# Expert stage as one row of 256-token blocks: nine fixed, the rest read from a table made on the chip

## The chip, the cores and the metric

The kernel runs on one core of one Trainium2 chip. The metric is the device time of one execution in microseconds (us). Three executions of the kernel before took 937.12, 929.86 and 933.24 us, median 933.24 us. Engine names are those of the profile: PE (matrix products; PEld is its weight load), DVE (vector), ACT (scalar), POOL (the engine that also issues gathers and scatters), SP (the queue that issues plain transfers).

## What is computed

```python
# 1: a recurrent layer over 768 steps (4 x 8 heads of 48), output x of 3072 tokens x 384
# 2: x = relu(x @ w_in) ** 2 @ w_out                       (384 -> 2048 -> 384)
# 3: the expert layer
skip_score = x @ w_skip
do_compute = skip_score > 0
out = x.copy()
xc = x[do_compute]
logits = xc @ w_gate                                       # 8 experts
e_idx = np.argmax(logits, axis=1)
gate_w = softmax(logits)[arange, e_idx]
for e in range(8):
    mask = e_idx == e
    h = np.maximum(xc[mask] @ w1[e], 0.0)                  # 384 -> 1024
    y[mask] = gate_w[mask, None] * (h @ w2[e])             # 1024 -> 384
out[do_compute] = xc + y
```

How many tokens an expert gets is known only on the chip. With the inputs of this case the eight experts get 1155, 132, 435, 318, 112, 43, 143 and 59 tokens, worked out from the reference; the other 675 of 3072 are passed through.

## The kernel before, in words

The first 651 us are the recurrent layer and the dense layer, laid over each other; the change leaves their code alone. While the dense layer runs, each token is routed: its number and its gate are scattered to a list per expert in memory (`lst`, two halves, merged by `merge` into `lsb` on the chip). The first entries of expert 0's list are read early (`lsp`), so that its first block can start before the lists are whole.

The expert stage works on **blocks**. A block is one expert's weights times up to 256 (`body256`) or 128 (`body128`) tokens of its list. Its parts:

- `gather`: POOL fetches the tokens' rows of x by index, 128 at a time, into `xg`. `xprep` turns them round on PE and splits them into a high and a low part (ACT the high, DVE the low).
- `l1(f)`, f = 0 to 7: nine products of 256 columns (three passes over high and low parts) into one of four PSUM banks; ACT makes the relu, DVE the low part of the hidden values (`gl`). `l2(f)`: for each half of the tokens three products of 384 columns into `acc[t]`. `l2(f)` stands four steps behind `l1`.
- `finish`: DVE multiplies by the gate and adds x (`yo`), POOL scatters the rows to `out`.
- The weights: SP loads an expert's weights as eight pieces of 384 KB into `raw` (`ew_load`), and ACT or DVE with DVE or POOL split each piece into high and low (`ew_split`). There are two sets of split weights and two `raw` buffers. While a block of expert e runs, the weights of e + 1 are split and those of e + 2 loaded, piece by piece at places that the table `CTP` sets.

Which blocks run is decided at run time: after each block every engine tests the expert's count (`large`, line 949: is there another 256; `level`, line 956: more than 128 left or not). The first block of expert 0 is outside these tests. With the counts above the order is: expert 0 five blocks of 256; expert 1 one; expert 2 two; expert 3 one of 256 and one of 128; experts 4 and 5 one of 128 each; expert 6 one of 256; expert 7 one of 128. So ten blocks of 256 and four of 128. At the very end a flag is tested (line 991) that redoes two blocks of expert 0 if the early list was not whole; with these inputs it is not set.

Of the kernel before, what the change touches and what calls it, by code (L numbers as in the profile page):

```python
# [83 lines left out]
def rwkv_moe_kernel(ctx: ExitStack, tc: tile.TileContext, a_in, v_in, ud, wio,  # L84
# [7 lines left out]
    xtd = dram.tile([NB * 4, 96, S], F32, name="xtd")  # L92

# [31 lines left out]
    flg = per.tile([1, 2], I32, name="flg")  # L125
# [496 lines left out]
    def ew_piece(e, k):  # L622

        r = raws[e > 0 and e % 2 == 0][:, k]
        w1h, w1l, w2h, w2l = ew[e % 2]
        if k < 4:
            s = slice(256 * k, 256 * k + 256)
            return r, r.rearrange("p (k f) -> p k f", k=KC), w1h[:, :, s], w1l[:, :, s]
        s = slice(2 * (k - 4), 2 * (k - 4) + 2)
        return r, r.rearrange("p (j d) -> p j d", j=2), w2h[:, s], w2l[:, s]  # L630

    def ew_load(e, k):
        nc.sync.dma_start(raws[e > 0 and e % 2 == 0][:, k], we[e, k])

    def ew_split(e, k, eng, dv=0):
        _, r, h, l = ew_piece(e, k)
        (nc.vector.tensor_copy if dv else nc.scalar.copy)(h, r)  # L637
        eng.tensor_tensor(l, r, h.bitcast(F32), ALU.subtract)
# [93 lines left out]
    NLV = NTOK // UT  # L732
    xgs = [[cp.tile([128, DM], F32, name=f"xg0_{t}") for t in range(2)]]
    yos = [cp.tile([128, DM], F32, name=f"yo{i}") for i in range(2)]
    ptx = [ptk, pu]
    nyo = [0]
    xhs, xls = list(xth), list(xtl)

    def xbuf(e, k):
        return 2 if k % 2 else e % 2  # L740

    def gbuf(e, k):
        return 3 if k % 2 else e % 3

    def ids(e, k, t):
        c = e * LB + 2 * k + t
        return lsb[:, c, 0:1], lsb[:, c, 1:2].bitcast(F32)

    def ids0(e, k, t):
        return lsp[0][:, 2 * k + t, 0:1], lsp[0][:, 2 * k + t, 1:2].bitcast(F32)  # L750
# [9 lines left out]
    def gather(e, k, idf=ids):  # L760
        for t in range(2):
            nc.gpsimd.indirect_dma_start(
                xgs[gbuf(e, k)][t], None, x2d[:, :],
                bass.IndirectOffsetOnAxis(ap=idf(e, k, t)[0], axis=0),
                bounds_check=NTOK + PADR - 1, oob_is_err=False)

    def xprep(e, k, t):
        i = xbuf(e, k)
        bank = ptx[t]
        for kc in range(KC):  # L770
            nc.tensor.transpose(bank[:, kc * 128:(kc + 1) * 128], xgs[gbuf(e, k)][t][:, kc * 128:(kc + 1) * 128], ident)
        s = slice(t * 128, t * 128 + 128)
        src = bank[:, 0:DM].rearrange("p (k t) -> p k t", k=KC)
        nc.scalar.copy(xhs[i][:, :, s], src)
        nc.vector.tensor_tensor(xls[i][:, :, s], src, xhs[i][:, :, s].bitcast(F32), ALU.subtract)

    def finish(e, k, t, idf=ids):
        ix, gt = idf(e, k, t)
        y = yos[nyo[0] % len(yos)]
        nyo[0] += 1  # L780
        nc.vector.scalar_tensor_tensor(y, acc[t][:, 0:DM], gt, xgs[gbuf(e, k)][t], ALU.mult, ALU.add)  # L781
        nc.gpsimd.indirect_dma_start(  # L782
            out[:, :], bass.IndirectOffsetOnAxis(ap=ix, axis=0), y, None,
            bounds_check=NTOK - 1, oob_is_err=False)
# [6 lines left out]
    at(TB + 10, 3, lambda: gather(0, 0, ids0))  # L791
    for t in range(2):
        at(TB + 13 + t, 1, lambda t=t: xprep(0, 0, t))
# [7 lines left out]
    xls.append(cq.tile([128, KC, UT], F32R, name="cxl2"))  # L801
    hps = pgs + [[cq.tile([128, UT], F32R, name=f"{n}{i}") for n in ("gh", "gl")] for i in range(NPB, LAG + 1)]
    ls2 = cq.tile([128, NE * LB, 2], I32, name="ls2")
    hrs = cq.tile([128, FE], F32, name="hr")
    hth, htl = ([hps[d][z].rearrange("p (j t) -> p j t", j=2) for d in range(4)] for z in range(2))
    pb = [t.rearrange("p (j t) -> p j t", j=4)
          for t in (pat.rearrange("p a b c -> p (a b c)"), py.rearrange("p a b -> p (a b)"))]
    l1b = [ph[0], ph[1], pat.rearrange("p a b c -> p (a b c)"), py.rearrange("p a b -> p (a b)")]

    def hook(side, n):  # L810
        for v, m in sorted((v, m) for m, (v, _) in enumerate(side) if n <= v < n + 1):
            side[m][1]()

    def body256(e, k, side, idf=ids):

        w1h, w1l, w2h, w2l = ew[e % 2]
        xh, xl = xhs[xbuf(e, k)], xls[xbuf(e, k)]
# [13 lines left out]
        def l2(f):  # L831
            hh, hl = hps[f % (LAG + 1)]
            for t in range(2):
# [16 lines left out]
        for t in range(2):  # L850
            finish(e, k, t, idf)

    def body128(e, k, side):
        w1h, w1l, w2h, w2l = ew[e % 2]
        xh, xl = xhs[xbuf(e, k)], xls[xbuf(e, k)]

        def l1(z, ns):
            s = slice(512 * z, 512 * z + 512)
            for n in ns:
                kc, (a, w) = n % 3, ((xh, w1h), (xh, w1l), (xl, w1h))[n // 3]  # L860
                nc.tensor.matmul(ph[z], a[:, kc, 0:128], w[:, kc, s], start=(n == 0), stop=(n == 3 * KC - 1))
            if ns[-1] == 3 * KC - 1:
                nc.scalar.activation(hrs[:, s], ph[z], AF.Relu)

        def turn(z):
            for j in range(4):
                f = 4 * z + j
                nc.tensor.transpose(pb[j // 2][:, j % 2], hrs[:, f * 128:(f + 1) * 128], ident)
            for m in range(2):
                d = 2 * z + m  # L870
                src = pb[m][:, 0:2]
                (nc.vector.tensor_copy if d == 1 else nc.scalar.copy)(hth[d], src)
                nc.vector.tensor_tensor(htl[d], src, hth[d].bitcast(F32), ALU.subtract)

        def l2(f):
            for n, (a, w) in enumerate(((hth, w2h), (hth, w2l), (htl, w2h))):
                nc.tensor.matmul(acc[0][:, 0:DM], a[f // 2][:, f % 2], w[:, f, :],
                                 start=(f == 0 and n == 0), stop=(f == NJE - 1 and n == 2))

        hook(side, 0)  # L880
        l1(0, range(0, 9))
        hook(side, 1)
        l1(1, range(0, 5))
        turn(0)
        hook(side, 2)
        l1(1, range(5, 9))
        hook(side, 3)
        l2(0)
        l2(1)
        turn(1)  # L890
        hook(side, 4)
        l2(2)
        hook(side, 5)
        l2(3)
        l2(4)
        hook(side, 6)
        for f in range(5, 8):
            l2(f)
        hook(side, 7)
        finish(e, k, 0)  # L900

    def sides(e, k, full):
        side = []

        def add(v, f):
            side.append((v, f))

        if full and k + 1 < NLV:
            add(CTP["g"][2], lambda: gather(e, k + 1))
            add(4, lambda: hint(f"n{e}_{k}", counts[e] > UT * (k + 1)))  # L910
        if k == 0 and e + 2 < NE:
            add(CTP["g"][full], lambda: gather(e + 2, 0))
        if k == 0 and e + 1 < NE:
            splits(side, e + 1, int(full))
        if e + 1 < NE:
            add(3.5, lambda: hint(f"s{e + 1}_0", counts[e + 1] > 128))
        for t in range(2):
            if k == 0 and e + 1 < NE:
                add(CTP["x"][full][t], lambda t=t: xprep(e + 1, 0, t))
            if (e, k) == (0, 1):  # L920
                add(CTP["x"][1][t], lambda t=t: xprep(1, 0, t))
            if full and k + 1 < NLV:
                add(CTP["x"][2][t], lambda t=t: xprep(e, k + 1, t))
        return side

    def splits(side, e, m):
        for p in range(8):
            def f(p=p):
                ew_split(e, p, nc.gpsimd if CTP["e"][m][p] else nc.vector, CTP["h"][m][p])
                if e + 2 < NE and m < 2:  # L930
                    ew_load(e + 2, p)
            side.append((CTP["l"][m][p], f))
            if m == 2:
                side.append((0.01, lambda p=p: ew_load(2, p)))
                side.append((max(4, CTP["l"][m][p] + 0.001), lambda p=p: ew_load(3, p)))
# [145 lines left out]
```

## Time and profile before

| | |
|---|---|
| median of three runs | 933.24 us (929.86 to 937.12) |
| the profiled execution | 937.27 us, its span 935.4 us, so 1.9 us lie outside the span |
| PE busy | 825.9 us, 88% of the span |
| DVE, ACT, POOL busy | 562.7, 450.6, 558.3 us |
| mean granted PE clock | 0.968 of full |
| expert stage on PE | 651.0 to 920.5 us |

The span runs from the first to the last instruction. A busy PE is not PE at its peak, so a block is best measured from the start of its first product to the start of the next block's. "PEclk" in a window is the clock granted to PE as a share of full: it has two levels, 1.2 and 2.4 GHz, and a value between is a mix over the window.

### The profile page before, as it was taken

Reading aid. Unit: us, or ns where it says so; the run is one execution under the profiler, and the core shown is the slowest. Engines: PE = TensorE matmul, PEld = TensorE weight load, DVE = VectorE, ACT = ScalarE, POOL = GpSimd, SP = SyncE. Lnnn points to the kernel's source line nnn. Section 1 sums busy time; section 2 is a strip of 40 time slices with the busy share of each in tenths; the row PEclk is TensorE's granted clock in tenths of the full one; section 3 lists DMA queues with packets and bytes.
Section 4 is the critical chain, followed back from the end, with each engine's and each line's share of the span. In section 5 each row is a group of like instructions: output and inputs, shape, how many; then the busy total and the mean of one; then the engine's idle time right before and its main releaser. Section 6 shows DMA issues by size and latency. Waiting matters only on the chain. (4 is left out here: it accounts for less than half of the span.)

```text
span 935.4 us, 17875 instructions
## 1 busy us (share of the span) xinstructions
PE 825.9 (88%) x6528; PEld 774.8 (83%) x6528; DVE 562.7 (60%) x1222; ACT 450.6 (48%) x1160; POOL 558.3 (60%) x603
## 2 busy tenths in 40 slices
PE   2574899999999999999999999989989989897873
PEld 2454788999999999999999999988979978886773
DVE  6986962658576767666667676325622357265651
ACT  1342565665656656666566556556312233144330
POOL 7765876767676767667676767335741254254440
PEclk9999999999999999999999999989999998999787
DMA  7454322232223131313232311055921145253310
GB/s 191 144 171 117 131 59 51 77 76 76 68 59 84 43 84 43 85 42 85 43 84 47 94 36 48 11 189 167 308 88 49 35 153 185 69 185 102 99 32 6
DMA packets 56639, 86.84 MB, mean 93 GB/s; under 512 B 31476, under 2 KB 40840, under 8 KB 56480
## 3 DMA queue, kind: packets, MB, share of 16 engines
q1 hardware_dynamic: 49104, 72.53, 27.2%
q0 software_dynamic: 4736, 11.18, 3.8%
q10 hardware_dynamic: 2640, 1.23, 0.6%
q8 instruction: 72, 1.18, 0.5%
q14 instruction: 87, 0.71, 0.3%
HBM read 68.44 MB, written 15.16 MB: 89 GB/s over the span
## 5 line engine op out<-in xcount | busy, mean ns | idle before, releaser
L364 POOL TENSOR_TENSOR gl<-g,gh 128x256 fp32r<-128x256 f32 x192 | 149.3, 779 | 144.4 <-ACT gh L363 99.7
L356 PE MATMUL ph<-xt,wih 128*128 128x256 f32 x1152 | 228.6, 294 | 4.2 <-PEq L719 3.8
L356 PEld LDWEIGHTS ph<-xt,wih 128*128 128x128 f32 x1152 | 184.6, 193 | 8.6 <-issue 4.3
L356 PE MATMUL ph<-xt,wil 128*128 128x256 f32 x576 | 164.2, 285 | 0.0
L372 PE MATMUL acc<-woh,gl 128*128 128x394 f32 x384 | 132.7, 346 | 0.7 <-POOL gl L364 0.7
L372 PE MATMUL acc<-woh,gh 128*128 128x394 f32 x384 | 133.0, 346 | 0.0
L361 ACT ACTIVATE g<-ph 128x256 f32<-128x256 f32 x192 | 72.8, 379 | 124.7 <-PE ph L356 97.3
L372 PE MATMUL acc<-wol,gh 128*128 128x394 f32 x384 | 131.0, 341 | 0.0
L356 PEld LDWEIGHTS ph<-xt,wil 128*128 128x128 f32 x576 | 111.0, 193 | 0.0
L287 DVE COPY_PREDICATED gr<-cis,pat 64x256 f32<-64x256 int32 x192 | 85.5, 445 | 32.9 <-PE pat L277 28.7
L782 POOL DMA_INDIRECT out<-yo,lsb x22 | 22.7, 1033 | 111.5 <-DVE yo L781 71.6
L362 ACT ACTIVATE g<-g 128x256 f32<-128x256 f32 x192 | 80.2, 418 | 6.1
L363 ACT CAST gh<-g 128x256 fp32r<-128x256 f32 x192 | 77.9, 406 | 6.1
L372 PEld LDWEIGHTS acc<-woh,gl 128*128 128x128 f32 x384 | 72.3, 188 | 4.2 <-POOL gl L364 3.9
L372 PEld LDWEIGHTS acc<-woh,gh 128*128 128x128 f32 x384 | 72.7, 189 | 0.7
L372 PEld LDWEIGHTS acc<-wol,gh 128*128 128x128 f32 x384 | 72.9, 190 | 0.0
L277 PE MATMUL pat<-ru,kbd 112*128 112x128 f32 x384 | 56.6, 295 | 14.7 <-POOL kbd L250 14.5
L277 PEld LDWEIGHTS pat<-ru,kbd 112*128 112x128 f32 x384 | 53.9, 209 | 15.2 <-POOL kbd L250 14.5
L221 DVE STREAM_TRANSPOSE knd<-kbd 32x256 f32<-32x256 f32 x144 | 62.4, 434 | 3.5 <-POOL kbd L250 1.1
L250 POOL TENSOR_TENSOR kbd<-ain,bsc 48x512 f32<-48x512 f32 x48 | 59.2, 1233 | 3.2 <-DVE bsc L215 0.7
L836 PE MATMUL acc<-w2h,gh 128*128 128x384 f32 x160 | 57.5, 359 | 0.0
L329 PEld LDWEIGHTS py<-gr,vz 128*64 128x64 f32 (+2 forms) x768 | 33.5, 144 | 28.0 <-ACT vz L320 12.8
(214 smaller groups left out, 1781.0 us busy)
## 6 DMA issues: line engine op xcount, KB each, us to landing
raw<-in_we SPq DMA_DIRECT2D x64, 384.0 KB
ain<-in_a_in SPq DMA_DIRECT2D x23, 675.9 KB
raw<-in_wio SPq DMA_DIRECT2D x16, 768.0 KB
vz<-in_v_in SPq DMA_DIRECT2D x44, 128.0 KB
x2d<-x SPq DMA_DIRECT2D x12, 384.0 KB
out<-x SPq DMA_DIRECT2D x12, 384.0 KB
xt<-yt SPq DMA_DIRECT2D x72, 32.0 KB
ain<-in_a_in ACTq DMA_DIRECT2D x1, 675.9 KB
```

What stands on the lines that cost most here:

```text
L221: nc.vector.transpose(kn[64 * h + 32 * b2:64 * h + 32 * b2 + 32, :, :, 64 * h + 32 * a:64 * h + 32 * a + 32], kb[64 * h + 32 * a:64 * h + ...
L250: eng("lk", H).tensor_tensor(st["kb"][sl, :, :, 64 * h:64 * h + 64], k[sl], st["rc"][sl], ALU.mult)
L277: nc.tensor.matmul(pat[:, c], kb[0:112, qq, c, :], ru[:, qq, c], start=True, stop=True)
L287: nc.vector.copy_predicated(gr[sl, qq, :, h, :], msk[sl].unsqueeze(1).to_broadcast([64, 4, CH]), pat[sl, :, m, :])
L329: nc.tensor.matmul(py[64 * h:64 * h + 64, P % 2, c * CH:(c + 1) * CH], hv[H][ks, qq, c, h, :], gr[ks, qq, c, h, :], start=True, stop=True)
L356: nc.tensor.matmul(h[:, 0:UT], w[:, kc, j * 128:(j + 1) * 128], x[:, kc, :], start=(n == 0), stop=(n == 3 * KC - 1))
L361: nc.scalar.activation(g, h[:, 0:UT], AF.Relu)
L362: nc.scalar.activation(g, g, AF.Square)
L363: nc.scalar.copy(gh, g)
L364: nc.gpsimd.tensor_tensor(gl, g, gh.bitcast(F32), ALU.subtract)
L372: nc.tensor.matmul(acc[t][:, 0:OW], a[:, s], w[:, j, :], start=(j == 0 and n == 0), stop=(j == NJ - 1 and n == 2))
L836: nc.tensor.matmul(acc[t][:, 0:DM], a[:, s], w[:, f, :], start=(f == 0 and m == 0), stop=(f == NJE - 1 and m == 2))
```

## The change

The branches on every expert's count go. The expert stage becomes one row of blocks, all of 256 tokens. Nine are fixed: two of expert 0 (from the early list) and one of each other expert. All that is left over (`rest`) is up to twelve further blocks; a table of their expert and list place is computed by 25 small DVE operations in block 1 (`table`), and block n of the rest runs if the table has more than n entries. The test stands nested, one level deeper for each block, and is true for five blocks with these counts: experts 0, 0, 0, 2, 3.

The weights of block n + 1 are always split during block n and those of block n + 2 always loaded, for the rest with the expert's number read from the table into a register of SP, so expert 0's weights are loaded and split three times more. The last four `l2` steps of a block are now done for the first 128 tokens, then for the second, so that the first half can be finished earlier; the second half's scatter waits until the next block in the fixed row. `xg`, x and `yo` take turns by block number. The order of loads in block 0 changes: the lists first, then the eight pieces of the second weight set.

```diff
 CTP = {
-    "l": [[0, 0.1, 0.2, 1.7, 2.2, 3.2, 4.5, 5.5], [0.4, 1.2, 2.0, 2.8, 3.6, 4.4, 5.2, 6.0],
...
+    "l": [0.3, 1.2, 2.1, 3.0, 3.9, 4.4, 5.9, 6.7],
+    "e": [0, 1, 0, 0, 1, 0, 1, 0],
+    "x": [5.1, 5.6],
+    "s": 1.6,
+    "g": 2.6}
+NX = NTOK // UT
+NST = NE + 1
...
+    def ew_load(n, k, ex=None):
+
+        src = we[n, k] if ex is None else we[bass.ds(ex, 1), k].rearrange("o p f -> (o p) f")
+        nc.sync.dma_start(raw(n)[:, k], src)
...
-        (nc.vector.tensor_copy if dv else nc.scalar.copy)(h, r)
+        nc.scalar.copy(h, r)
         eng.tensor_tensor(l, r, h.bitcast(F32), ALU.subtract)
...
+    def wset(n):
+
+        return max(n - 1, 0)
+
+    def ids(n, t):
+        if n < 2:
+            l = lsp[0][:, 2 * n + t]
+        elif n < NST:
+            l = lsb[:, (n - 1) * LB + t]
+        else:
+            l = idt[:, n - NST, t]
+        return l[:, 0:1], l[:, 1:2].bitcast(F32)
...
+    def table():
+
+        V = nc.vector
...
+        V.tensor_scalar(ti[:, 0], cnt[0:1], 1, None, ALU.subtract)
+        V.tensor_scalar(ti[:, 1], ti[:, 0], 8, None, ALU.arith_shift_right)
...
+        V.tensor_tensor_scan(cx, cfs[0:1, 256:256 + NE], ex, 0.0, ALU.mult, ALU.add)
+        V.tensor_copy(nbk, cx[:, NE - 1:NE])
...
+        V.tensor_copy(tbl[:, 0], eb)
+        V.tensor_copy(tbl[:, 1], kb)
+
+    def ex_load(b):
+        exr[b] = nc.values_load(tbl[0:1, 0, b:b + 1], engines=[mybir.EngineType.SP], min_val=0, max_val=NE - 1)
+
+    def id_load(b):
+        c = nc.values_load(tbl[0:1, 1, b:b + 1], engines=[mybir.EngineType.SP], min_val=0, max_val=NE * LB - 2)
+        nc.sync.dma_start(idt[:, b], lm[:, bass.ds(c, 2), :])
...
-        for f in range(NJE + LAG):
-            if f < NJE:
-                steps.append(lambda f=f: l1(f))
+        for f in range(NJE):
+            steps.append(lambda f=f: l1(f))
             if f >= LAG:
                 steps.append(lambda f=f - LAG: l2(f))
+        for t in range(2):
+            for f in range(NJE - LAG, NJE, 2):
+                steps.append(lambda f=f, t=t: (l2(f, (t,)), l2(f + 1, (t,))))
...
-    def body128(e, k, side):
...
+            finish(n, t)
+            if t == 0 or n >= NST - 1:
+                scatter(n, t)
...
+        if 0 < n < NST:
+            add(CTP["s"], lambda: scatter(n - 1, 1))
+        if n + 2 <= last and n > 0:
+            add(CTP["g"], lambda: gather(n + 2))
+        if n < last:
+            for t in range(2):
+                add(CTP["x"][t], lambda t=t: xprep(n + 1, t))
+        w = wset(n) + 1
+        if n and n < last:
+            for p in range(8):
+                add(CTP["l"][p], lambda p=p: ew_split(w, p, nc.gpsimd if CTP["e"][p] else nc.vector))
+        if n and wset(n) + 3 <= last - 1:
+            q = w + 2
+            if q >= NE:
+                add(0.01, lambda: ex_load(q - NE))
+            for p in range(8):
+                add(CTP["l"][p] + 0.02, lambda p=p: ew_load(q, p, exr[q - NE] if q >= NE else None))
+        if 2 <= n < 6:
+            for b in range(3 * n - 6, 3 * n - 3):
+                add(7 + 0.1 * (b % 3), lambda b=b: id_load(b))
...
-    def large(e, k):
-        body256(e, k, sides(e, k, True))
-        if k + 1 < NLV:
-            with tc.If(counts[e] > UT * (k + 1), label=f"n{e}_{k}"):
-                level(e, k + 1)
...
+    side = sides(0) + [(0.6, r3), (0.61, r3b), (0.62, r2c), (0.625, r2d), (0.63, r4), (0.64, lists),
+                       (6.1, merge_all), (6.3, lambda: gather(2))]
+    side += [(0.65, lambda p=p: ew_load(2, p)) for p in range(8)]
...
+    block(0, side)
+    block(1, sides(1) + [(6.9, table)])
+    for n in range(2, NST):
+        block(n, sides(n))
+    nblk = nc.values_load(nbk[0:1, 0:1], min_val=0, max_val=NX)
+
+    def rest(n):
+        with tc.If(nblk > n - NST):
+            block(n, sides(n))
+            if n + 1 < NST + NX:
+                rest(n + 1)
+
+    rest(NST)
```

Three places of the new order, as the built program has them (line numbers here are those of the changed file).

On PE, the end of the last fixed block and the start of the first of the rest. L879 are the `l2` products, L867 the `l1` products; `acc_73` is the second half of the tokens.

```order
L879 MATMUL acc_73<-w2h_12690,gh_118 128x384
L879 MATMUL acc_73<-w2l_12691,gh_118 128x384
L879 MATMUL acc_73<-w2h_12690,gl_119 128x384
L950 TENSOR_LOAD nbk
L953 COMPARE_AND_BRANCH
L867 MATMUL ph_70<-xt_107,w1h_6783 128x256 x3
L867 MATMUL ph_70<-xt_107,w1l_6784 128x256 x3
```

One register load and one test stand where the kernel before has a test of line 949, and the block's products follow the test directly; the four later tests of the rest have the same form without the register load.

On DVE, the end of block 1 and the start of block 2. L640 is the low part of a weight piece, L775 that of the next block's tokens, L778 the finish, L872 the low part of a hidden step (`gl`).

```order
L775 TENSOR_TENSOR cxl_12700<-pu,cxh_12699 128x3x128
L640 TENSOR_TENSOR w2l_12691<-raw_6782,w2h_12690 128x768
L817 TENSOR_TENSOR tx<-cn_92,cnt 1x1
L818 SCALAR_TENSOR_TENSOR tx<-cn_92,tx 1x1
...
L847 CAST tbl<-tv 1x12
L848 CAST tbl<-tv 1x12
L778 SCALAR_TENSOR_TENSOR yo_0_12703<-acc_72,lsp_89,xg_0_12693 128x384
L778 SCALAR_TENSOR_TENSOR yo_1_12704<-acc_73,lsp_89,xg_1_12694 128x384
L872 SCALAR_TENSOR_TENSOR gl_115<-ph_70,gh_114 128x256
L640 TENSOR_TENSOR w1l_6784<-raw_12692,w1h_6783 128x3x256
L872 SCALAR_TENSOR_TENSOR gl_117<-ph_71,gh_116 128x256
```

The 25 rows of the table (L817 to L848) stand between the last weight piece of block 1 and its two finishes, and ahead of the first `gl` of block 2.

On SP, inside the rest: the loads of one block and the test ahead of the next.

```order
L629 ISA
L629 DMA raw_12692<-in_we 128x768
L953 COMPARE_AND_BRANCH
L851 TENSOR_LOAD tbl
L851 ISA x2
L629 ISA
L629 DMA raw_6782<-in_we 128x768
```

Each load of the rest has an address instruction (ISA) ahead of it, and each block one register load from the table; loads of both `raw` buffers take turns.

## Rows read from the trace of the kernel before

**Rows 1.** Starts of blocks, PE timeline, no idle before: start us, us, engine, line, operation.

```profile
650.99 0.52 PE L824 MATMUL ph<-xt,w1h 128*128 128x256 f32 x3
669.86 0.51 PE L824 MATMUL ph<-cxh,w1h 128*128 128x256 f32 x3
694.32 0.40 PE L824 MATMUL ph<-xt,w1h 128*128 128x256 f32 x2
711.84 0.52 PE L824 MATMUL ph<-cxh,w1h 128*128 128x256 f32 x3
729.36 0.52 PE L824 MATMUL ph<-xt,w1h 128*128 128x256 f32 x3
796.10 0.40 PE L824 MATMUL ph<-cxh,w1h 128*128 128x256 f32 x2
884.41 0.52 PE L824 MATMUL ph<-xt,w1h 128*128 128x256 f32 x3
```

**Rows 2.** Starts of blocks after idle time, PE timeline; in brackets idle us and releaser.

```profile
748.39 0.59 PE L824 MATMUL ph<-xt,w1h 128*128 128x256 f32 x3 [1.33 <-PEq L949]
771.30 0.98 PE L824 MATMUL ph<-xt,w1h 128*128 128x256 f32 x3 [4.38 <-DVEq L949]
817.50 0.59 PE L824 MATMUL ph<-xt,w1h 128*128 128x256 f32 x3 [3.68 <-DVEq L949]
839.04 0.93 PE L861 MATMUL ph<-w1h,cxh 128*128 128x512 f32 x3 [1.52 <-issue]
851.81 0.95 PE L861 MATMUL ph<-w1h,xt 128*128 128x512 f32 x3 [3.35 <-issue]
871.32 1.62 PE L861 MATMUL ph<-w1h,xt 128*128 128x512 f32 x3 [2.75 <-issue]
908.45 1.62 PE L861 MATMUL ph<-w1h,xt 128*128 128x512 f32 x3 [5.69 <-issue]
```

**Rows 3.** Waits inside blocks and the products after one, PE timeline.

```profile
689.03 0.87 PE L771 MATMUL ptk<-cfs,xg 128*128 128x128 f32 x3 [4.39 <-DMA xg<-x2d,lsb]
...
790.68 0.55 PE L771 MATMUL ptk<-cfs,xg 128*128 128x128 f32 x3 [1.97 <-DVE xt L775]
790.98 0.52 PE L836 MATMUL acc<-w2h,gh 128*128 128x384 f32 x1
...
794.50 0.38 PE L836 MATMUL acc<-w2h,gh 128*128 128x384 f32 x1
```

**Rows 4.** The tests of line 949 on PE: count, least/median/most ns.

```profile
L949 PEldq COMPARE_BRANCH  x13: 65/193/4592, 690.7 to 903.3; - x13
```

**Rows 5.** Two stretches: us, busy us by engine, PEclk, DMA share, GB/s.

```profile
651.00:670.00 19.00, 17.99 (x132) 17.80 (x131) 15.21 (x43) 8.60 (x18) 10.00 (x8) 1.00 0.84 292
...
887.00:904.00 17.00, 15.76 (x112) 15.33 (x110) 14.23 (x20) 7.99 (x16) 9.41 (x6) 1.00 0.11 30
```

**Rows 6.** First and last of eight dependent small operations, DVE timeline.

```profile
651.39 0.17 DVE L400 TENSOR_REDUCE mx<-lg 128x2 f32<-128x16 f32 x1
...
652.85 0.16 DVE L413 TENSOR_TENSOR cum<-cum,ohb 128x8 bf16<-128x8 bf16 x1
```

**Rows 7.** Weight pieces' low parts by line: count, least/median/most ns.

```profile
L638 DVE TENSOR_TENSOR w2l<-raw,w2h x18: 940/1144/4278, 635.0 to 899.2; 128x768 fp32r<-128x768 f32 x18
...
L638 POOL TENSOR_TENSOR w1l<-raw,w1h x12: 1815/1858/2100, 632.3 to 891.4; 128x768 fp32r<-128x768 f32 x12
```

**Rows 8.** The end, timeline of all engines.

```profile
920.13 0.34 PE L877 MATMUL acc<-w2h,gl 128*128 128x384 f32 x1
920.51 0.62 DVE L781 SCALAR_TENSOR_TENSOR yo<-acc,lsb,xg 128x384 f32<-128x384 f32 x1 [2.19 <-PE acc L877]
921.40 0.97 POOL L782 DMA_INDIRECT out<-yo,lsb  x1 [11.37 <-DVEq L991]
```

**Rows 9.** The two scatters of one block, POOL timeline.

```profile
694.89 1.01 POOL L782 DMA_INDIRECT out<-yo,lsb  x1 [6.78 <-DVE yo L781]
698.30 1.00 POOL L782 DMA_INDIRECT out<-yo,lsb  x1 [2.39 <-DVE gl L829]
```

More of the change, by code (lines that the diff above doesn't have):

```diff
@@ L801, in rwkv_moe_kernel @@
     xls.append(cq.tile([128, KC, UT], F32R, name="cxl2"))
+    yos = [[cq.tile([128, DM], F32, name=f"yo{i}_{t}") for t in range(2)] for i in range(2)]
     hps = pgs + [[cq.tile([128, UT], F32R, name=f"{n}{i}") for n in ("gh", "gl")] for i in range(NPB, LAG + 1)]
     ls2 = cq.tile([128, NE * LB, 2], I32, name="ls2")
[L804 to L807, printed above, removed]
@@ L808, in rwkv_moe_kernel @@
-    l1b = [ph[0], ph[1], pat.rearrange("p a b c -> p (a b c)"), py.rearrange("p a b -> p (a b)")]
[L810 to L817, printed above, removed]
+    idt = cq.tile([128, NX, 2, 2], I32, name="idt")
+    tx = cq.tile([1, 4, NE], F32, name="tx")
+    ti = cq.tile([1, 2, NE], I32, name="ti")
@@ L819, in l1, with block @@
+    def ex_load(b):
[3 more added lines that the diff above has]
+        nc.sync.dma_start(idt[:, b], lm[:, bass.ds(c, 2), :])
+    def block(n, side):
+        w1h, w1l, w2h, w2l = ew[wset(n) % 2]
+        xh, xl = xhs[n % 3], xls[n % 3]
         def l1(f):
@@ L829, in l1, with l2 @@
             nc.vector.scalar_tensor_tensor(hl, h, 0.0, hh.bitcast(F32), ALU.max, ALU.subtract)
-        def l2(f):
+        def l2(f, ts=(0, 1)):
             hh, hl = hps[f % (LAG + 1)]
-            for t in range(2):
+            for t in ts:
                 s = slice(t * 128, t * 128 + 128)
@@ L850, in body256 @@
         for t in range(2):
-            finish(e, k, t, idf)
-    def body128(e, k, side):
[L854 to L900, printed above, removed]
@@ L902, in sides @@
-    def sides(e, k, full):
-        side = []
+            finish(n, t)
+            if t == 0 or n >= NST - 1:
+                scatter(n, t)
+    def sides(n):
+        side, last = [], NST + NX - 1
         def add(v, f):
             side.append((v, f))
[L908 to L923, printed above, removed]
-        return side
@@ L926, in splits @@
[L926 to L935, printed above, removed]
-    def hint(label, cond):
-        tc.mark_branch_hint_location(label, hint=cond)
@@ L966, in lists, with merge_all @@
         nc.sync.dma_start(ls2, lv[1])
-    def flag():
-        nc.vector.tensor_tensor(flg[:, 0:1], cn0[0:1, 0:1], cnt[0:1, 0:1], ALU.is_lt)
-        nc.vector.scalar_tensor_tensor(flg[:, 1:2], cn0[0:1, 0:1], float(2 * UT), flg[:, 0:1], ALU.is_lt, ALU.mult)
-    side = [(0.6, r3), (0.61, r3b), (0.62, r2c), (0.625, r2d), (0.63, r4), (0.64, lists),
-            (5.1, lambda: merge(lsb, ls2)), (5.3, flag), (7.4, lambda: hint("n0_0", counts[0] > UT)),
-            (7.8, lambda: gather(1, 0)), (7.9, lambda: gather(2, 0))]
-    side += [(5.6 + 0.5 * t, lambda t=t: xprep(0, 1, t)) for t in range(2)]
-    side += [(3.2 + 0.5 * e, lambda e=e: load_count(e)) for e in range(NE)]
-    splits(side, 1, 2)
+    def merge_all():
+        merge(lsb, ls2)
+        nc.sync.dma_start(lm, lsb)
+    side = sides(0) + [(0.6, r3), (0.61, r3b), (0.62, r2c), (0.625, r2d), (0.63, r4), (0.64, lists),
+                       (6.1, merge_all), (6.3, lambda: gather(2))]
+    side += [(0.65, lambda p=p: ew_load(2, p)) for p in range(8)]
     r1()
@@ L980, in rwkv_moe_kernel @@
     r2b()
-    gather(0, 1, ids0)
-    body256(0, 0, side, ids0)
-    with tc.If(counts[0] > UT, label="n0_0") as c:
-        level(0, 1)
-    with c.Else():
-        for t in range(2):
-            xprep(1, 0, t)
-    for e in range(1, NE):
-        level(e, 0)
-    fv = nc.values_load(flg[0:1, 1:2], min_val=0, max_val=1)
-    with tc.If(fv > 0):
-        gather(0, 0)
-        for p in range(8):
-            ew_load(0, p)
-            ew_split(0, p, nc.gpsimd if p % 3 == 2 else nc.vector)
-        for t in range(2):
-            xprep(0, 0, t)
-        body256(0, 0, [])
-        with tc.If(counts[0] > UT):
-            gather(0, 1)
-            for t in range(2):
-                xprep(0, 1, t)
-            body256(0, 1, [])
+    gather(1)
+    block(0, side)
[9 more added lines that the diff above has]
+    rest(NST)
 def layout(inputs):
```

100 lines of the change are left out of this document (51 added, 49 removed), and 5 rows, old and new, of the table CTP.

## The prediction

> **What bounds the kernel now.** I read the PE timeline first, because PE is busy 88% of the span, and looked for where one block begins and the next begins. Where nothing waits, a block of 256 tokens takes 17.52 us: 694.32 to 711.84 and 711.84 to 729.36 [rows 1]. PE is never idle there, so the block cannot be shorter with the same products. Then I read the starts that have idle time before them: seven blocks begin after 1.33 to 5.69 us of idle [rows 2], each at a place where the engines had left a nest of tests or come into or out of a block of 128. Two more waits lie inside blocks, 4.39 us for a gather and 1.97 us for DVE [rows 3]. After the longer ones the clock is lower: the triple of products at 771.30 lasts 0.98 us, that at 748.39 only 0.59, and the products from 790.98 to 794.50 last 0.52 before falling to 0.38 [rows 2, 3]. These are the levels of 1.2 and 2.4 GHz. It stayed high after 1.33 and 1.52 us of idle (0.59, and 0.93 against 1.62 for the larger triples) and fell after 1.97 and 4.38 [rows 2, 3].
>
> So the expert stage, 650.99 to 920.47 us, 269.5 us [rows 1, 8], is PE-bound in a good part and latency-bound at its joints. Its lengths in order, as differences of the starts: 18.87, 24.46, 17.52, 17.52, 19.03, 22.91, 24.80, 21.40, 21.54, then 12.77, 19.51 and 13.09 (blocks of 128), 24.04, and 12.02 (128) [rows 1, 2, 8].
>
> **The change, part by part.**
>
> *Blocks of 128 become blocks of 256.* Four blocks now take 12.77 + 19.51 + 13.09 + 12.02 = 57.4 us; at 17.52 each they are 70.1. Cost 12.7.
>
> *The joints go.* The nine blocks of 256 behind block 0 take 193.2 us; at 17.52 they are 157.7. Gain 35.5. That holds if the next block's tokens and weights are always ready. For the weights there is one full precedent: the block from 884.41 splits a whole set, and in the stretch 887 to 904 PE was busy 15.76 us, that is without a break to its end at 902.8, with DVE busy 14.23, ACT 7.99 and POOL 9.41 of 17 [rows 5]. The changed block moves three casts from DVE to ACT, which leaves both below the block's length. Block 0 stays at 18.87: its wait for the count is still there.
>
> *The tests.* The rest has five tests that are true, and the block follows each in the code. Tests of this form that were true cost PE 65 ns, the least of the 13 [rows 4]: at 694.32, 711.84 and 729.36 a block began behind one with no idle [rows 1]. The dear ones, up to 4.6 us, are the false ones, where PE must go elsewhere. The one false test left comes after the last product. Cost on the path 0; POOL has to get through it before the end, as it has to now at lines 956 and 991. What the price would be if true tests behaved like false ones is the first rival below.
> The Trainium skill ("Runtime: NRT & Kernel Launch", Instruction fetch mechanics) says a taken branch with a target outside the fetched pages stalls for a fetch, and gives this as a reason why control flow at run time is expensive. The trace agrees for the false tests and shows nothing for the true ones; by the page's general warning each of the five would be charged, by the rows none is.
>
> *Reloads.* Each block asks for eight pieces of 384 KB and moves four gathers or scatters of 196 KB: 3.9 MB in 17.52 us, 224 GB/s. The stretch 651 to 670 moved 292 GB/s at a DMA share of 0.84 [rows 5], so the share would be 0.64. A piece is asked for two blocks before it is split: cost 0. Loads whose address is in a register are not in the trace; between nothing and some 2 us each (8 x 2 is still less than a block) they hide in SP, which does nothing else. I take 0.
>
> *The table.* 25 small operations on DVE. Eight dependent ones started 1.46 us apart from first to last, 0.21 us each [rows 6], so 5.2 us. They stand behind the last weight piece of block 1, which is placed at 6.7 of 8, about 14.7 us into the block; with its cast and 1.14 us on DVE [rows 7] it is done at about 16.7. Table to 21.9, two finishes of 0.62 [rows 8] to 23.1, then the first `gl` of block 2, about 6.0 us into that block. What is queued behind it: the fifth `l1` needs the bank that this `gl` empties. A block is sixteen steps of 2304 columns, 1.07 us each, so PE comes there at 4.3: idle 1.7 to 1.8 us, and at that length the clock may fall, which costs the 3.5 us from 790.98 to 794.50 at half pace, 1.8 us [rows 3]. I take 3.6. Bounds: 0 if DVE is less behind than I reckon; 7.0 if all 5.2 us show and the clock falls.
>
> *Block 0.* The gather for block 2 is issued in block 0 and needed some 12 us into block 1. Before, the gather of 689.03 was issued only in block 1. The lists come ahead of the bulk loads in SP's queue, the bulk loads later by as much and not needed until block 2. Cost 0, with a rival.
>
> *The end.* Now 0.93 us from the last product to the scatter, then 14.0 us to the end of the span [rows 8]. Afterwards the last block has two scatters, and the second follows the first by at least 3.41 us [rows 9], since it waits for it. The first can start some 1.2 us before the last product ends if DVE is free, or just after if it is behind the last weight piece: the second then starts 2.2 to 3.5 us after the last product instead of 0.93. Cost 2.0 (bounds 0 and 4.0, one more such wait). The useless splits and loads for blocks that do not come end inside the 14 us.
>
> **The sum**, on the profiled execution: -35.5 + 12.7 + 3.6 + 2.0 = -17.2 us; 937.3 becomes 920.0. The median of the runs is 4.0 us below that execution, so I forecast 916.0 us against 933.24, 1.8% faster.
>
> **Rivals.**
>
> 1. *The true tests cost what false ones cost* (the other side). The place is PE at the start of each of the five blocks of the rest. Price: 4.38 us of idle as at 771.30, the joint behind a full block [rows 2], and 1.8 us of low clock, 31 us in all: 947 us. For it: nothing prefetches the block, and the nest is new code. Against it: 65 ns [rows 4], three times without idle [rows 1]. It decides from about 3.4 us per test on, where the whole gain is gone. Chance 6%.
>
> 2. *DVE becomes the bound because POOL holds it up* (also the other side). A low part on DVE lasts 0.94 us at best and 4.28 at worst, on POOL 1.86 [rows 7]. Every changed block has three of POOL's and five of DVE's, and four gathers or scatters of 1.0 us [rows 8, 9]. It decides when DVE is held 3.3 us longer per block than in the stretch from 887, since 14.23 + 3.3 is the block [rows 5]. At 2 us more than that, PE idles 2 us in each of twelve blocks and runs low for 3.5: 12 x 3.8 = 46, giving 962. Against it: in that stretch PE lost nothing. Chance 5%.
> The Trainium skill ("GPSIMD Engine Reference", 1. Specifications) says that engine's memory interfaces are shared with the vector engine and contended when the latter reads two operands there, as all five low parts do. The trace's 4.28 us agrees. Taken for every one of POOL's operations that rule gives this rival's price, by the row of that stretch the price is 0.
>
> 3. *The start still waits*: the gather for block 2 comes late and block 1 takes 24.46 us again [rows 1]: 6.9 more, 923. For it: the merge of the lists still waits for the last scatter to them. Chance 8%.
>
> 4. *The row is longer than I count*: the table yields one more block, or late weights cost as much in sum: 17.5 more, 933, no change. Chance 5%.
>
> **How the numbers follow.** The forecast's own range: best 937.3 - 22.8, less 4.0 for the runs, 910; worst (7.0 and 4.0) 921, and the runs before spread by 4 us either way. It has 72%; 4% I keep for a better result, where block 0 shortens too. The range 907 to 927 takes in the forecast and rival 3, about 8 in 10. About 1% is what a measurement of this kernel can tell from no change, so faster means below 923.9 and slower above 942.6: 0.78, 0.11 and 0.11.
>
> **What would show it.** Starts of blocks 17.5 us apart from 669.9 on, and the last product near 901 instead of 920; a clock of 1.00 in all but perhaps one stretch; one wait on PE of about 2 us at the fifth `l1` of block 2, released by DVE; tests of some 70 ns on PE at the five blocks of the rest; a share of DMA near 0.6. The forecast is wrong if PE waits at a joint of the rest for a test, for a split or for a token gather, if DVE's low parts rise well above 1.14 us in the middle, or if there are not fourteen blocks.

## The result, and the profile after it

The changed kernel takes 923.14 us (median of 4 runs, 921.21 to 924.09), the kernel before 934.37 (4 runs): ratio 0.9882, interval 0.9837 to 0.9927, so 1.2% faster. The profiled executions stand at 921.21 and 937.27 us, a span of 919.4 against 935.4: 16.0 us less there, 11.2 in the medians.

The PE timeline, read as in [rows 1, 2] (start us, us, engine, line, operation; in brackets idle us and releaser): starts of blocks and the last product, of after.

```profile
650.79 0.52 PE L867 MATMUL ph<-xt,w1h 128*128 128x256 f32 x3
...
669.75 0.52 PE L867 MATMUL ph<-xt,w1h 128*128 128x256 f32 x3
...
687.41 0.52 PE L867 MATMUL ph<-cxh,w1h 128*128 128x256 f32 x3
...
693.01 0.62 PE L867 MATMUL ph<-cxh,w1h 128*128 128x256 f32 x3 [1.14 <-DVE gl L872]
...
696.51 0.63 PE L867 MATMUL ph<-cxh,w1h 128*128 128x256 f32 x3 [1.10 <-DVE gl L872]
...
707.78 0.52 PE L867 MATMUL ph<-xt,w1h 128*128 128x256 f32 x3
...
813.57 0.52 PE L867 MATMUL ph<-xt,w1h 128*128 128x256 f32 x3
...
831.24 0.52 PE L867 MATMUL ph<-xt,w1h 128*128 128x256 f32 x3
...
901.59 0.34 PE L879 MATMUL acc<-w2h,gl 128*128 128x384 f32 x1
```

No block start has idle time in front of it, where seven had it [rows 2]. From 669.75, where block 1 starts, to the end of the last product at 901.93 are 232.18 us: block 2 takes 20.37, the other twelve 17.65 on average (17.59 to 17.68; the last, to the end of its last product, 17.83). The only waits of PE behind block 0 are the two of block 2.

All waits of PE from the start of block 0 to the last product, of after (us in total, times, longest); the second row lies in block 0:

```profile
PE ph L867 <- DVE gl L872: 2.2, 2, 1.1
PE pu L759 <- DVE cum L442: 1.0, 1, 1.0
```

The tests around the blocks of the rest, on PE (count, least/median/most ns), which answer to [rows 4]:

```profile
L953 PEldq COMPARE_BRANCH  x7: 65/65/5732, 811.4 to 904.7; - x7
```

The five true ones take 65 to 80 ns. The 5732 is the sixth, false one, which stands behind the last product in the code; a seventh row of 203 ns follows it.

Two windows, as in [rows 5] (us, busy us by engine, PEclk, DMA share, GB/s), and the low parts, as in [rows 7]:

```profile
651.00:670.00 19.00, 17.99 (x132) 17.83 (x131) 9.19 (x39) 4.69 (x13) 6.10 (x6) 1.00 0.63 208
833.00:850.00 17.00, 17.00 (x123) 16.97 (x122) 13.97 (x17) 9.23 (x17) 9.60 (x8) 1.00 0.69 226
```

```profile
L640 DVE TENSOR_TENSOR w1l<-raw,w1h x42: 941/959/3244, 626.2 to 893.0; 128x768 fp32r<-128x768 f32 x42
L640 DVE TENSOR_TENSOR w2l<-raw,w2h x29: 958/1980/3067, 634.9 to 899.8; 128x768 fp32r<-128x768 f32 x29
L640 POOL TENSOR_TENSOR w2l<-raw,w2h x27: 1832/1847/1888, 640.6 to 899.1; 128x768 fp32r<-128x768 f32 x27
```

A block of the rest is PE without a break, DVE busy 14 of 17 us, at full clock, with 226 GB/s beside it (the sum on record had 224). The median low part of `w2l` on DVE rose to 1.98 us, from 1.14 [rows 7].

What DVE and POOL do around the two waits of block 2 (timelines, columns as for PE):

```profile
685.42 1.97 DVE L640 TENSOR_TENSOR w2l<-raw,w2h 128x768 fp32r<-128x768 f32 x1 [0.91 <-ACT w2h L639]
...
691.40 0.16 DVE L848 CAST tbl<-tv 1x12 int32<-1x12 f32 x1
691.49 1.14 DVE L778 SCALAR_TENSOR_TENSOR yo<-acc,lsp,xg 128x384 f32<-128x384 f32 x2
692.54 0.41 DVE L872 SCALAR_TENSOR_TENSOR gl<-ph,gh 128x256 fp32r<-128x256 f32 x1
692.88 3.24 DVE L640 TENSOR_TENSOR w1l<-raw,w1h 128x768 fp32r<-128x768 f32 x1
696.04 0.41 DVE L872 SCALAR_TENSOR_TENSOR gl<-ph,gh 128x256 fp32r<-128x256 f32 x1
```

```profile
693.44 1.85 POOL L640 TENSOR_TENSOR w1l<-raw,w1h 128x768 fp32r<-128x768 f32 x1
```

The table's last operation (its first started at 687.32) ends at 691.56, the two finishes follow, and the first `gl` frees PE at 693.01. The low part behind it lasts 3.24 us and ends 0.8 after POOL's, and the next `gl` frees PE at 696.51.

The end, all engines, as in [rows 8]:

```profile
901.67 1.13 DVE L778 SCALAR_TENSOR_TENSOR yo<-acc,idt,xg 128x384 f32<-128x384 f32 x2
902.56 1.02 POOL L781 DMA_INDIRECT out<-yo,idt  x1 [1.62 <-DVE yo L778]
906.97 1.00 POOL L781 DMA_INDIRECT out<-yo,idt  x1 [3.39 <-DVEq L953]
```

From the last product to the end of the span are 17.5 us, where there were 15.0. The second scatter starts 4.41 us after the first; its row names DVE's sequencer, but the first lands at 906.17, and wherever the traces of this kernel and its variants have the landing, the second starts 0.8 us after it.

### The profile page after: what moved, and what is told of

Same layout as the page of the kernel before. It is cut to its first block, busy times and chain, and to the rows that moved or that the text cites. A ratio compares the mean times of both kernels' runs of the same rounds, so it can differ in the third digit from the quotient of the medians.

```text
span 919.4 us, 18685 instructions
## 1 busy us (share of the span) xinstructions
PE 840.1 (91%) x6790; PEld 798.0 (87%) x6790; DVE 608.6 (66%) x1273; ACT 495.1 (54%) x1229; POOL 585.8 (64%) x618
## 5 line engine op out<-in xcount | busy, mean ns | idle before, releaser
L879 PE MATMUL acc<-w2h,gh 128*128 128x384 f32 x224 | 77.7, 347 | 0.0
L879 PE MATMUL acc<-w2l,gh 128*128 128x384 f32 x224 | 75.3, 336 | 0.0
L879 PE MATMUL acc<-w2h,gl 128*128 128x384 f32 x224 | 75.3, 336 | 0.0
L640 DVE TENSOR_TENSOR w2l<-raw,w2h 128x768 fp32r<-128x768 f32 x29 | 63.3, 2182 | 18.0 <-ACT w2h L639 15.5
L640 POOL TENSOR_TENSOR w2l<-raw,w2h 128x768 fp32r<-128x768 f32 x27 | 49.9, 1849 | 30.4 <-ACT w2h L639 30.0
```

Source lines behind the costliest of these rows:

```text
L879: nc.tensor.matmul(acc[t][:, 0:DM], a[:, s], w[:, f, :], start=(f == 0 and m == 0), stop=(f == NJE - 1 and m == 2))
```

## The experiments

Theory: the idle time at the joints of before belongs to its tests, true tests are free, and the table is the whole of the stall in block 2. Main rival: the joints belong to the unequal blocks themselves. The stage is measured from the start of block 1 to the end of the last product: 250.61 us before [rows 1, 8], 232.18 after. In the second trace of the changed kernel and in two variants that leave the stage alone it comes out at 232.17 or 232.18 again, so that one trace settles tenths there. It does not for the end: from the last product to the end of the span the two traces of the changed kernel have 17.5 and 18.6 us.

**1. The kernel before without its tests.**

```
-        with tc.If(counts[e] > UT * k + 128) as c:
-            large(e, k)
-        with c.Else():
-            body128(e, k, sides(e, k, False))
+        if HAVE[e] > UT * k + 128:      # HAVE: this input's counts
+            large(e, k)
+        else:
+            body128(e, k, sides(e, k, False))
```
(and the same for `n{e}_{k}` and `n0_0`; the last two tests are left out with the blocks that they guard, and so are the branch hints (`hint`) and the register loads of the counts)

> The kernel before with the same blocks in the same order (ten of 256, four of 128), but the path fixed in the code from this input's counts: no tests, no branches; it computes this input's result only. Theory (the idle time at the joints belongs to the tests: an engine that takes the other branch is late, and no work is prefetched across it): the 22.7 us of idle before seven starts go, and with them some 5 us of low clock; the 4.4 us wait for a gather in the second block and the 2 us wait for DVE stay. About 907 us, 25 to 29 below before. Rival (it belongs to the unequal blocks themselves: gathers and weight pieces placed too late around a block of 128): the waits come back as waits for DMA, DVE or ACT inside the blocks, and it gains less than 10 us, 925 to 934.

901.82 us against 936.15 (ratio 0.9639, 0.9612 to 0.9665): 34.3 us faster, 21 below the changed kernel. The stage takes 219.03 us, 31.6 less. All waits of PE in it and in block 0 (the row of `pu`), and the starts of its first two blocks:

```profile
PE acc L877 <- DVE gl L873: 9.2, 4, 3.4
PE ptk L771 <- DMA xg<-x2d,lsb: 4.5, 1, 4.5
PE pu L757 <- DVE cum L441: 1.0, 1, 1.0
PE ph L824 <- DVE cxl L775: 0.3, 1, 0.3
...
669.95 0.51 PE L824 MATMUL ph<-cxh,w1h 128*128 128x256 f32 x3
...
695.65 0.51 PE L824 MATMUL ph<-xt,w1h 128*128 128x256 f32 x3
```

Blocks of 128 wait for `gl` (9.2 us, where 4.2 were seen before), the gather is as late as in [rows 3]; no start of a block waits for a test or for `issue`. The theory holds, and it gained more than it said: the wait for DVE in [rows 3], which was to stay, is gone too, and the tests with their hints and loads were worth more than all that the change gained. The nine blocks of 256 behind block 0 lose 24.2 us (193.2 to 169.0), the four of 128 lose 7.4. The first of the nine loses nothing: it takes 25.70, as it still waits for its gather.

**2. The changed kernel without tests.**

```
-    rest(NST)                      # nested tc.If(nblk > n - NST)
+    for n in range(NST, NST + 5):
+        block(n, sides(n))
```

> The changed kernel with the five blocks of the rest written out, without a test (nothing else is changed; right for this input's count only). Theory (true tests cost nothing): starts of blocks 17.6 us apart as before, nothing gained up to the last product; at most the end is some 2 us shorter, since the false test and its waits are not there. 921 to 923 us. Rival (the tests hold the blocks back in a way that shows as longer products or later splits): blocks of the rest fall towards 17.52 and below, and over 3 us go.

918.82 us (ratio 0.9811, 0.9792 to 0.983). The stage is 232.17 us, with the same periods to 0.01: five true tests cost nothing. The end took 13.6 us instead of 17.5 (18.6 in the second trace of the changed kernel): the one false test costs some 4 to 5, twice what I expected. Behind the second scatter the span lasts 9.3 us instead of 12.5.

**3 to 5. One false test more in the row**, in front of the second block of the rest, around a body of two instructions, of one block, of five blocks.

```
         with tc.If(nblk > n - NST):
+            if n == NST + 1:
+                with tc.If(nblk > NX - 1):
+                    count(cnt)      # or: block(n - 1, []), once or five times
             block(n, sides(n))
```

> The changed kernel with one false test more, between the first and the second block of the rest (at about 831), around two instructions (one product, one copy). Theory (what the joints of the kernel before cost is the false test itself: engines leave the straight path and bring their semaphores level at the other end): PE idle of 1.3 to 5.7 us before that block, as at the seven joints of before, whatever the body's length. Rival (what costs is the distance that is jumped): under 0.5 us here, and some 4 us where a whole block is jumped.

> As the kernel with the small body, with a whole block of 256 tokens as the body of the false test. Theory (the test itself): the same idle time before the block as with the small body, within 1 us. Rival (the distance): 4 to 5.7 us, at least 3 more than with the small body.

> The changed kernel with the one false test more at about 831, now around five whole blocks of 256. With two instructions as the body that test kept PE 0.24 us, with one block 0.86. Theory (distance: the farther the place that PE goes on from, the longer the branch lasts): 3.3 to 5.3 us, as the false tests of the kernel before, which jump over seven blocks and more; PE idle of 1.5 us or more before that block. Rival (the number of tests nested, or which engine is late, sets it): below 1.5 us, as with one block.

They ran once each: 924.63, 925.67 and 932.14 us, beside 935.85 for the kernel before in the round of the first two and 935.38 in that of the third. The test on PE in the three kernels, and how the next block starts (PEq and DVEq are the engines' sequencers; "issue" is idle time in which the engine waited for nothing that the profile shows):

```profile
L955 PEldq COMPARE_BRANCH  x1: 238/238/238, 829.9 to 829.9; - x1
...
833.22 0.59 PE L867 MATMUL ph<-xt,w1h 128*128 128x256 f32 x3 [0.15 <-PEq L955]
```

```profile
L955 PEldq COMPARE_BRANCH  x1: 858/858/858, 829.4 to 829.4; - x1
...
833.61 0.60 PE L867 MATMUL ph<-xt,w1h 128*128 128x256 f32 x3 [1.08 <-DVEq L955]
```

```profile
L955 PEldq COMPARE_BRANCH  x1: 4767/4767/4767, 831.7 to 831.7; - x1
...
836.86 0.59 PE L867 MATMUL ph<-xt,w1h 128*128 128x256 f32 x3 [2.00 <-PEq L955]
...
841.84 0.54 PE L867 MATMUL pat<-xt,w1h 128*128 128x256 f32 x2 [2.47 <-issue]
...
842.82 0.84 PE L867 MATMUL pat<-xt,w1h 128*128 128x256 f32 x3
```

The two blocks around the test are longer than in the changed kernel by 0.4, 1.3 and 6.4 us in sum. My theory, that a false test costs the same whatever it skips, fell; the rival of distance stands, though one block cost less than it said. Beyond five blocks the branch lasts 4.77 us, of which 2.00 show as idle time; PE runs dry once more, 2.5 us after it arrives, and then works at half pace (0.84 instead of 0.52 for a triple; the granted clock from 842.8 to 846.0 is 0.57). The false tests of before jump over at least that much code: the dear ones lasted 2.8 to 5.3 us on PE, among them one of 4.69 that takes up most of the 5.69 us of idle in [rows 2]. The Trainium skill ("Runtime: NRT & Kernel Launch", Instruction fetch mechanics) says that a taken branch stalls for a fetch when its target lies outside the instructions already there. The three runs agree: 0.24 and 0.86 us near, 4.77 far. The flag test of before (line 991), which jumps over two blocks, lies between them with 3.34 us on PE. Distance is not all, though: the last test row of the changed kernel lasted 203 ns on PE, its counterpart in the kernel of experiment 4 4888. Why is open.

**6. The loads of the rest left out.**

```
-                add(CTP["l"][p] + 0.02, lambda p=p: ew_load(q, p, exr[q - NE] if q >= NE else None))
+                if q < NE:
+                    add(CTP["l"][p] + 0.02, lambda p=p: ew_load(q, p))
```
(and the register loads of the expert's number go)

> The changed kernel without the loads of weights for the rest: the splits stay and work on old data, so the result of the blocks of the rest is not the reference's. Theory (the loads are hidden, and only lengthen a block from 17.52 to 17.62 by traffic): blocks from the sixth on 17.52 apart, about 0.8 us in all; the second scatter at the end starts some 1 us sooner, since no bulk transfer stands beside the first. Rival (loads hold up splits or products): over 2 us up to the last product.

919.95 us in one run. The stage is 232.18 us, every period as before: the loads are hidden altogether, and the 0.1 us by which a block is longer than 17.52 is not theirs; what it is stays open. The second scatter follows the first by 3.62 us instead of 4.41, and the end takes 16.6 us. The expectation puts that down to the loads, but the traces do not bear it out: the changed kernel's second trace has 5.44 us with the same loads, and the kernel of experiment 2, which keeps them, has 3.69, with 272 GB/s moved from the first scatter's start to its landing (41 in this run). Its two scatters:

```profile
904.02 1.02 POOL L781 DMA_INDIRECT out<-yo,idt  x1 [1.62 <-DVE yo L778]
907.71 0.99 POOL L781 DMA_INDIRECT out<-yo,idt  x1 [2.67 <-DMA out<-yo,idt]
```

What sets the time that the first scatter needs to land stays open.

**7. The table twice.** `block(1, sides(1) + [(6.9, table), (6.9, table)])`

> The changed kernel with the table's 25 operations made twice at the same place. Theory (they stand in DVE's queue ahead of the finishes, and nothing hides what is over the 2 us of slack): PE idle in block 2 grows by the table's own 4.2 us, to 5.4 for the first wait, block 2 to 24.6 us, and at that length the clock falls, which adds up to 1.8 us. Rival (some of it is hidden again by slack later in the block): block 2 below 23 us.

927.29 us in one run. Block 2 takes 25.46 us, 5.1 more for 4.2 us of table. PE waits once, 5.3 us. The theory holds: nothing hides the second table. Windows of the changed kernel (first row) and of this one (columns as in [rows 5]):

```profile
692.00:697.80 5.80, 3.68 (x25) 3.37 (x26) 5.80 (x9) 1.40 (x3) 4.57 (x4) 1.00 0.23 61
```

```profile
692.00:697.80 5.80, 0.50 (x5) 0.30 (x3) 5.25 (x31) 0.86 (x2) 0.69 (x1) 0.85 0.00 0
697.70:701.50 3.80, 3.76 (x15) 3.76 (x16) 3.80 (x4) 1.10 (x2) 3.26 (x3) 0.50 0.14 52
```

After 5.3 us of idle the granted clock is 0.50, the lower of its two levels; after 1.14 and 1.10 us it stayed at 1.00.

**8. The table handed out**, one operation at a time from 2.6 to 6.4 of block 1.

```
-    block(1, sides(1) + [(6.9, table)])
+    table()      # now only fills the list tops
+    block(1, sides(1) + [(2.6 + 0.158 * i, f) for i, f in enumerate(tops)])
```

> The changed kernel with the 25 operations of the table handed out one by one over block 1, from 2.6 to 6.4 of 8, instead of together at 6.9. Theory (the table is the whole of the stall, because it stands ahead of the finishes and the first low part of block 2): no PE wait in block 2, its length 17.6 instead of 20.4, 2.8 us gone, near 920.3. Rival (DVE has no such room in block 1, or POOL holds it up at that place anyway): the wait moves to the token preparation of block 1 or to the start of block 2, or the second wait of 1.1 us stays, and 0 to 1.7 us are gained.

921.09 us (ratio 0.9837, 0.9814 to 0.986). Block 2 is 17.59 and no longer waits; block 1 grows from 17.66 to 18.04. The stage is 229.77, 2.4 less: the theory's 2.8, less 0.4.

**9. The first half finished early.**

```
         for m, f in enumerate(steps):
             f()
+            if m == len(steps) - 3:
+                finish(n, 0)
+                if n >= NST - 1:
+                    scatter(n, 0)
...
```

> The changed kernel with the first half's finish (and its scatter, from block 8 on) right after the step that completes it, two steps before the block's end and ahead of the last weight piece on DVE. Theory (the end hangs on the second scatter, which waits for the first): the first scatter starts at about 901 instead of 902.6, behind POOL's last weight piece, the second 4.4 later at about 905.4 instead of 907.0; 1.6 us gone, near 921.5. Rival (the end hangs on the false test, which engines pass at 904.7 to 906.5): less than 0.5 us.

920.42 us (ratio 0.9829, 0.9809 to 0.9849), but for another reason than expected. The stage lost 1.5 us, since one finish less stands behind the table (one wait of 0.74 in block 2); the end did not become shorter, 17.9 us:

```profile
897.33 1.55 POOL L781 DMA_INDIRECT out<-yo,idt  x1 [0.16 <-issue]
898.20 0.62 DVE L778 SCALAR_TENSOR_TENSOR yo<-acc,idt,xg 128x384 f32<-128x384 f32 x1 [0.21 <-PE acc L879]
903.68 0.99 POOL L781 DMA_INDIRECT out<-yo,idt  x1 [4.81 <-DMA out<-yo,idt]
```

The first scatter starts before the last product ends (898.16), and the second only 6.35 us after it, where the two traces of the changed kernel have 4.41 and 5.44: it still waits for the first to land, at 902.88.

**10 to 12. The changed kernel again, and two joined versions.** Both take the early finish, the table from 2.0 to 5.0 of block 1 and the count for the table at 3.1 of block 0; the second also moves loads:

```
-            for p in range(8):
+            for p in range(4):
                 add(CTP["l"][p] + 0.02, lambda p=p: ew_load(q, p, exr[q - NE] if q >= NE else None))
+        if n > 1 and wset(n - 1) + 3 <= last - 1:
+            o = wset(n - 1) + 3
+            for p in range(4, 8):
+                add(0.005, lambda p=p: ew_load(o, p, exr[o - NE] if o >= NE else None))
```

> The changed kernel again, unaltered, for its time beside the kernel before in more runs. Theory (the profiled pair showed the true difference, 16.0 us by its stages, and the runs differ in the part ahead of the stage, which both share): ratio near 0.983 to 0.986. Rival (the first ratio, 0.988, is right, and the profiled execution of before was a slow one): 0.988 or more.

> The changed kernel with the table handed out over block 1 (from 2.0 to 5.0), the first half finished two steps earlier, and the count for the table at 3.1 of block 0 instead of at its start. Theory: 2.8 us of stall in block 2 and the 1.0 us wait in block 0 go, the end stays at 17.5 to 17.9 us: 3.8 us less than the changed kernel, 0.4% of its time. Rival (the handed-out table or the later count makes new waits): 2.4 us or less.

> The same with the loads of the last four pieces of a set put at the start of the next block, so that nothing but the scatters moves at the end of the last block. Theory (the early first scatter took 5.6 us to land because bulk loads for blocks that do not come stood beside it): it lands in about 3.5 us, the second scatter starts at 0.5 to 2.5 us after the last product instead of 5.5, the end takes 15 to 16 us instead of 17.9; about 6 us less than the changed kernel. Rival (the end hangs on what engines do at the false test, not on the scatter): the end stays above 17 us.

The changed kernel again: 923.64 us against 935.38, ratio 0.9879 (0.9845 to 0.9913): the rival's number, though the interval takes in the theory's upper end; the stage again 232.17.

Joined: 922.14 us (0.9853, 0.9822 to 0.9883). The waits in block 0 and block 2 are gone, but block 1 takes 21.72 us. DVE and POOL in it:

```profile
680.00 0.40 DVE L874 SCALAR_TENSOR_TENSOR gl<-pat,gh 128x256 fp32r<-128x256 f32 x1
680.33 2.46 DVE L841 TENSOR_TENSOR tv<-tv 1x12 f32<-1x12 f32 x1
682.82 0.16 DVE L842 TENSOR_SCALAR tv<-tv 1x12 f32<-1x12 f32 x1
...
684.11 1.77 DVE L846 TENSOR_SCALAR tv<-tv 1x12 f32<-1x12 f32 x1
...
686.26 0.41 DVE L874 SCALAR_TENSOR_TENSOR gl<-py,gh 128x256 fp32r<-128x256 f32 x1
```

```profile
680.91 1.85 POOL L640 TENSOR_TENSOR w2l<-raw,w2h 128x768 fp32r<-128x768 f32 x1
683.80 2.05 POOL L640 TENSOR_TENSOR w2l<-raw,w2h 128x768 fp32r<-128x768 f32 x1 [1.04 <-ACT w2h L639]
```

Operations on twelve numbers, 0.16 us elsewhere, last 2.46 and 1.77 us and end 0.03 and 0.02 us after POOL's low part. These two of the table's operations are held by POOL, the `gl` behind them comes late, and PE waits 2.33 us for it. The rival was right.

With the loads moved: 920.73 us (0.984, 0.9811 to 0.9868), block 1 still 20.43. The second scatter starts 5.38 us after the first (6.35 in experiment 9), with only 30 GB/s moved in all from the first's start to its landing (227 in experiment 9); the end takes 16.9 us, 1.0 less than in experiment 9. That is half or less of what I expected and no more than the two traces of the changed kernel differ by, so a gain from the loads is not shown. 8, 9 and this one all lie some 2 to 3 us below the changed kernel, which their intervals do not separate from it, and the gains do not add up; the version that is far ahead, that of experiment 1, is right for one input only.

## Why the prediction was right, and by how much

Step by step, on the profiled executions:

- **Blocks of 128.** 4 x 17.65 less 57.4 is 13.2; the sum had 12.7.
- **Joints.** 193.2 becomes 9 x 17.65 = 158.9: 34.4, the sum had 35.5. The difference is a block of 17.65 for 17.52. Experiment 1 shows that tests were the cause of most of it: without them these nine blocks lose 24.2. Another 8.0 lie in block 1, which takes 25.70 there and 17.66 here. That is the gather, which POOL starts at 685.73 before, inside block 1, and at 667.40 now; no run moved it alone. The other 2 are spread over the other eight.
- **Tests.** Right: true ones cost nothing (experiment 2). That the dear ones are those where PE goes elsewhere is right too, and experiments 3 to 5 add that the distance counts.
- **Reloads.** Right: nothing (experiment 6). The share of DMA is 0.69, not 0.64.
- **Table.** 2.7 instead of 3.6. The step had two parts, 1.8 of idle and 1.8 of low clock. The clock did not fall. The idle time is 1.14 and then 1.10, and the second part I had not seen: the first low part of block 2 lasts 3.24 us on DVE, since POOL's scatter and, behind it, POOL's low part stand beside it. Two sizes were off by about 1 us and cancel: the table itself took 4.2 us, not 5.2, but the last weight piece ahead of it, held up by POOL (1.97 us on DVE, not 1.14), ended 17.6 us into block 1, not 16.7.
- **Block 0.** 18.96 after 18.87: nothing, as said.
- **End.** 2.5 instead of 2.0 (3.6 in the second trace). The wait of the second scatter is there, but that the size came out is in part luck: the second scatter starts 5.04 us after the last product, not 2.2 to 3.5, and from it to the end of the span are 12.5 us, not 14.0. The first start is late because the first scatter starts only 0.63 us after the last product and the second 4.41 after that, not 3.41. The false test costs some 4 to 5 us of the end (experiment 2); before had such tests there as well.

-34.4 + 13.2 + 2.7 + 0.1 + 2.5 = -15.9, against -17.2 on record; the spans differ by 16.0. Of the signs of being wrong one came true: the low parts of `w2l` on DVE rose from a median of 1.14 us to 1.98. It cost PE nothing except in block 2, so the sign was set too tight.

What was off is the level, 916.0 for 923.1. Of these 7.1 us, 1.2 are the sum's. The rest is the step from the profiled execution to the runs: I took 4.0 off because the first three runs of before had a median of 933.24; with the later ones it stands at 934.4 to 936.2, close to the profiled 937.27. The changed kernel's profiled execution in turn is 1.9 below its median. Where the executions differ the traces show in part: the same code ahead of the stage ends anywhere from 648.46 to 654.25 us in the twelve traces of the changed kernel and its variants, and the end of the changed kernel took 17.5 us in one and 18.6 in the other. Why is open; the gain of the medians, 11.2 and in the second round 11.7, is the one to go by.

The rivals: true tests cost like false ones: no. DVE bound because POOL holds it: POOL does hold it, in every block (1.98 and 2.4 us for 0.96), yet the block has room for it; it cost 1.1 us, in block 2, where the table had used up that room. Start still waits: no, block 1 takes 17.66; that its 923 is the number measured is chance. Row longer or weights late: no, fourteen blocks and no wait.

## What to carry to other kernels

Price a test by where it goes: one that falls through was free here, one that jumps over five blocks cost 6.4 us of the stage (experiment 5), and the joints of before had 1.3 to 5.7 us of idle time [rows 2], so lay the code out such that the usual path is the straight one, even at the price of padded work. Work that is queued on an engine in front of what frees a buffer is paid in full once the slack is used up, and small work put beside another engine's long operations may not be small. Take the level from many runs, not from one execution and three times.

## What the runs showed that was not expected

- A far branch costs twice: 4.77 us, 2.00 of them idle, and 2.47 us of dry PE 2.5 us after it arrived.
- A low part on DVE that is under way beside one on POOL ends only after it: in the changed kernel 32 of 33 ended 0.81 to 0.83 us after POOL's and took 1.37 to 3.24 us in all instead of 0.96 (the other one had nearly ended when POOL's began). Beside a scatter or a gather alone such a low part took its 0.96 (676.50, 714.52). Of the table's small operations two were caught, and ended 0.02 to 0.03 us after POOL's (2.46 and 1.77 us instead of 0.16). Operations that read one operand from PSUM are not held: all 20 `gl` that started or ran beside a POOL low part took their 0.42 us, such as this one.

```profile
674.39 1.84 POOL L640 TENSOR_TENSOR w1l<-raw,w1h 128x768 fp32r<-128x768 f32 x1 [3.30 <-ACT w1h L639]
674.69 0.42 DVE L872 SCALAR_TENSOR_TENSOR gl<-py,gh 128x256 fp32r<-128x256 f32 x1 [0.65 <-ACT gh L871]
```

The Trainium skill ("GPSIMD Engine Reference", 1. Specifications) has the interfaces contended where the vector engine reads two operands from SBUF or uses a mode with two ports. The low parts and L841 read two operands there, `gl` one, and L846 one; no run here tells which mode L846 ran in.

- The time that a scatter needs before the next can follow varies: the second could start 3.62 and 3.69 us after the first in two kernels (experiments 6 and 2), 4.41 and 5.44 in two traces of the changed one, 6.35 where the first was issued earlier (experiment 9). Loads beside it do not sort these numbers; the cause is open.
